# Expert products in one of four run-time widths, chosen by branches on TensorE

## The chip, the cores and the metric

The kernel runs on one core of a Trainium2 chip. The metric is device time in microseconds, lower is better; the time of the kernel before is the median of three runs. One more execution was recorded by the hardware profiler, and all rows below come from it.

## What is computed

A gated linear attention with a complex decay (4 batches, 8 heads, 768 steps, 48 values a head) gives 3072 rows of 384 values. A mixture of eight experts then takes each row to one expert, chosen by the largest of eight gate logits, and multiplies the expert's answer by two gates. The part that matters here:

```python
e_idx = np.argmax(logits, axis=1)
...
for e in range(E):
    mask = e_idx == e
    if not mask.any():
        continue
    h = np.maximum(x[mask] @ w1[e], 0.0)
    ye = h @ w2[e]
    out[mask] = gate_w[mask, None] * eom[mask, e, None] * ye
```

An expert has two matrices, `w1` of 384 x 1024 and `w2` of 1024 x 384. How many rows it gets is known only at run time.

## The kernel before

The program has two stages on one core. The first, the attention, lasts until some 278 us; it also routes the tokens. The second runs the eight experts one after the other (`experts`, L1125) and ends with the span.

**Places and capacities.** After most of the tokens are routed, the experts are ranked by how many tokens they have so far (`ranking`, L312), the fullest first. The expert at place n of this order gets room for `CAPS[n]` tokens (L24: 464, 440, 424, 416, 408, 400, 392, 384), whatever its number of tokens is in the end. Its tokens are gathered from DRAM into `rows` in four tiles (the last expert: three), so that token r of an expert lies in tile r mod 4. All products of place n stream `CAPS[n]` columns. `over` (L1390) compares the final counts with the capacities; if one is exceeded, a branch at the end of the program (L1411) enters a fallback, which the inputs here do not need. That branch is on all five engines, and each reads its word for it from `words` (L1410).

**One expert.** The 1024 hidden values are done in eight rounds `ft` of 128. Each float32 operand is split in a high and a low part, so a product is three matmuls on TensorE (high x high, low weight x high, high weight x low). A round has an up group, nine matmuls (3 x three parts of the 384 inputs) into one of two `up` banks (L1237), then ScalarE writes `hh` (relu, high part, L1241) and VectorE `hl` (low part, L1242). A down group of nine matmuls (L1174) adds the round into three `acc` banks; it is issued one round later, when `hh` and `hl` are there. After the eighth round the sums are copied to `yt`, and `put` (L1203) turns them back to rows: for each of four tiles three transposes into the single `yp` bank, `y` on ScalarE (times the gate, L1209), and an indirect DMA issued by GpSimd that scatters the rows (L1187). One tile is put in each of the next expert's rounds 1 to 4. The last expert computes its rows directly (`down_rows`, L1194), without `put`.

**Beside the products.** Each round also takes three steps of preparing the next expert (`ahead`, L1160): twelve steps split the weights, 128 x 512 each (ScalarE casts the high part, VectorE subtracts, L210 and L211), and wait for the weights' DMA through two `raw` buffers; three steps transpose the gathered rows into `xh` and `xl` (L1146 to L1148), in rounds 4 and 5.

**Order of work.** ScalarE and VectorE execute in the written order (`manual_schedule` with `by_hand`, L1408). The order on TensorE, SyncE and GpSimd in the expert stage is chosen by the framework's scheduler. In a round of the middle experts TensorE's order came out as up group, transposes if any, down group. In the written order a round has: up group, `hh`, `hl`, then one tile of `put` if there is one (L1244), the down group of the round before, then the three steps.

## Time and profile before

| what | value |
|---|---|
| median of 3 runs | 532.56 us (531.41 to 533.61) |
| profiled execution | 527.01 us |
| its span, first to last instruction | 525.3 us |
| TensorE matmuls busy | 489.0 us, 93% of the span |
| VectorE / ScalarE / GpSimd busy | 336.6 / 314.4 / 115.3 us |
| mean granted TensorE clock | 0.982 of full speed |

A busy share is a mean over stages with different limits. TensorE's matmuls are pipelined: one starts before the one ahead of it has ended, so what a matmul costs in a dense row is the distance between two starts, and a TensorE that is busy throughout can still be sped up by doing less. PEld is the loading of weights, which overlaps; PEldq, ACTq and the like are what an engine's sequencer does by itself, such as loads of registers and branches.

### The profile page before, as it was taken

The page shows a single profiled execution, that of the slowest core. Times are in us where ns is not written, and L with a number is a line of the kernel's source. Part 1 is how long each engine was busy: PE and PEld are TensorE (multiplying, and loading weights), DVE is VectorE, ACT ScalarE, POOL GpSimd, SP SyncE. Part 2 cuts the span into 40 slices and gives each one's busy share as a digit, 9 for nine tenths or more (in the row PEclk, how much of TensorE's full clock was granted, in tenths as well). Part 3 has the DMA queues.
Part 4 walks back from the last instruction along what each step waited for, and adds up shares of the span by engine and source line. Part 5 has one row for each costly group of instructions (what it writes and reads, how often), then busy time and mean ns, then how long its engine had stood idle before and what let it go on. Part 6 is the DMA issues. An engine that isn't in the chain of part 4 may idle for free.

```text
span 525.3 us, 10906 instructions
## 1 busy us (share of the span) xinstructions
PE 489.0 (93%) x4174; PEld 422.8 (80%) x4174; DVE 336.6 (64%) x777; ACT 314.4 (60%) x578; POOL 115.3 (22%) x134
## 2 busy tenths in 40 slices
PE   2799896999999999999999999999999999999992
PEld 0378574878777778778897889999999999999991
DVE  5679678979887988888867736354453636364220
ACT  7678677986869788756724436364453627264220
POOL 4002002020020203032320562413233322011112
PEclk9999989999999999999999999999999999999996
DMA  8764442526235321114425667445262635340001
GB/s 282 206 224 144 117 132 59 170 62 172 89 77 151 53 72 48 32 32 137 138 60 152 184 184 220 123 142 166 64 205 94 216 110 168 121 141 25 22 22 46
DMA packets 46898, 63.84 MB, mean 122 GB/s; under 512 B 11769, under 2 KB 38668, under 8 KB 46836
## 3 DMA queue, kind: packets, MB, share of 16 engines
q1 hardware_dynamic: 38708, 53.63, 33.7%
q0 software_dynamic: 8128, 9.42, 6.1%
q8 instruction: 35, 0.57, 0.5%
q14 instruction: 27, 0.22, 0.2%
HBM read 53.92 MB, written 9.88 MB: 121 GB/s over the span
## 4 chain that ended last, share of the span: by engine, by line
PE 65%; issue 16%; DVE 6%; ACT 5%; POOL 3%; DMA 3%; POOLq 0%; SPq 0%; DVEq 0%; ACTq 0%
PE up L1237 13%; PE acc L1174 12%; PE tr L94 7%; PE sc L664 6%; PE xo L678 4%; PE tr L245 4%; PE cs L574 4%; PE cs L521 3%; POOL out_dram L1187 3%; PE st L649 3%; PE xo L684 3%; PE st L644 1%; DMA carry<-ai 1%; DMA ar<-in_a_re_dram 1%; PE yp L94 1%
## 5 line engine op out<-in xcount | busy, mean ns | idle before, releaser
L1242 DVE SCALAR_TENSOR_TENSOR hl<-up,hh 128x464 fp32r<-128x464 f32 (+7 forms) x64 | 37.7, 590 | 72.8 <-ACT hh L1241 69.6
L1241 ACT ACTIVATE hh<-up 128x464 fp32r<-128x464 f32 (+7 forms) x64 | 33.0, 516 | 79.1 <-PE up L1237 76.4
L1237 PE MATMUL up<-xh,w1h 128*128 128x464 f32 (+7 forms) x192 | 68.7, 358 | 0.2 <-ACT xh L1024 0.2
L1237 PE MATMUL up<-xl,w1h 128*128 128x464 f32 (+7 forms) x192 | 67.7, 353 | 0.0
L1237 PE MATMUL up<-xh,w1l 128*128 128x464 f32 (+7 forms) x192 | 67.6, 352 | 0.0
L1174 PE MATMUL acc<-hh,w2h 128*128 128x464 f32 (+6 forms) x168 | 61.3, 365 | 0.0
L1174 PE MATMUL acc<-hl,w2h 128*128 128x464 f32 (+6 forms) x168 | 59.4, 353 | 0.0
L1187 POOL DMA_INDIRECT out_dram<-y,sid x28 | 31.7, 1133 | 125.7 <-ACT y L1209 122.7
L1174 PE MATMUL acc<-hh,w2l 128*128 128x464 f32 (+6 forms) x168 | 59.3, 353 | 0.0
L664 PE MATMUL sc<-qt,kt 96*128 96x128 f32 x384 | 52.5, 279 | 0.0
L664 PEld LDWEIGHTS sc<-qt,kt 96*128 96x128 f32 x384 | 47.2, 192 | 3.4 <-issue 1.8
L1118 POOL DMA_INDIRECT rows<-xd,sid x28 | 35.0, 1250 | 51.3 <-DVE hl L1242 25.7
L678 PE MATMUL xo<-scores,v 128*48 128x128 f32 x384 | 42.9, 278 | 0.3 <-issue 0.2
L211 DVE TENSOR_TENSOR w1l<-raw,w1h 128x512 fp32r<-128x512 f32 x48 | 30.7, 687 | 19.1 <-ACT w1h L210 19.1
L1064 POOL DMA_INDIRECT table<-entry,addr x20 | 27.0, 1348 | 53.0 <-DVE addr L1060 49.1
L544 POOL COPY rcs<-rcs 24x48 f32<-24x48 f32 (+2 forms) x10 | 6.0, 604 | 144.2 <-DMA rcs<-re 119.2
L211 DVE TENSOR_TENSOR w2l<-raw,w2h 128x512 fp32r<-128x512 f32 x48 | 30.6, 689 | 11.0 <-ACT w2h L210 10.8
L1237 PEld LDWEIGHTS up<-xl,w1h 128*128 128x128 f32 x192 | 36.1, 188 | 1.5 <-DVE xl L1025 0.4
L1237 PEld LDWEIGHTS up<-xh,w1h 128*128 128x128 f32 x192 | 36.1, 188 | 1.3 <-ACT xh L1024 0.4
L1237 PEld LDWEIGHTS up<-xh,w1l 128*128 128x128 f32 x192 | 36.2, 188 | 0.9
L684 PE MATMUL xo<-qt,state 96*48 96x128 f32 x320 | 36.5, 274 | 0.0
L665 DVE TENSOR_TENSOR scores<-sc,mask 128x512 f32<-128x512 f32 x48 | 32.7, 683 | 5.5 <-PE sc L664 5.1
(228 smaller groups left out, 1098.1 us busy)
## 6 DMA issues: line engine op xcount, KB each, us to landing
raw<-in_moe_w_dram SPq DMA_DIRECT2D x32, 768.0 KB
ar<-in_a_re_dram SPq DMA_DIRECT2D x24, 192.0 KB
ai<-in_a_im_dram SPq DMA_DIRECT2D x24, 192.0 KB
k<-in_k_dram SPq DMA_DIRECT2D x24, 192.0 KB
q<-in_q_dram SPq DMA_DIRECT2D x24, 192.0 KB
v<-in_v_dram SPq DMA_DIRECT2D x24, 192.0 KB
xd<-xn SPq DMA_DIRECT2D x24, 192.0 KB
rows<-xd,sid POOLq DMA_INDIRECT x28
```

Source lines behind the costliest of these rows:

```text
L94: return nc.tensor.transpose(out=out, in_=in_, identity=ident[p0:p0 + n, p0:p0 + n])
L211: nc.vector.tensor_tensor(out=lo[:, s], in0=raw[:, s], in1=hi[:, s].bitcast(F32), op=ALU.subtract)
L664: nc.tensor.matmul(sp[:, j * P:(j + 1) * P], r["kt"][:D2, h, :], r["qt"][:D2, h, :], start=True, stop=True)
L665: nc.vector.tensor_tensor(out=r["s"][:, 4 * hh:4 * hh + 4, :], in0=sp.rearrange("p (h t) -> p h t", t=P), in1=mask.unsqueeze(1).broadcast_ ...
L678: nc.tensor.matmul(op[u * DP:u * DP + D, j * P:(j + 1) * P], vt[c][:, h * D:(h + 1) * D], r["s"][:, h, :], start=True, stop=(cc == 0))
L684: nc.tensor.matmul(op[u * DP:u * DP + D, j * P:(j + 1) * P], xs[:D2, h * D:(h + 1) * D], r["qt"][:D2, h, :], start=False, stop=True)
L1118: ins = nc.gpsimd.indirect_dma_start(out=rows[e % 2][:n, i, :], out_offset=None, in_=xd[:known], in_offset=bass.IndirectOffsetOnAxis(ap=id ...
L1174: nc.tensor.matmul(accs[kt][:, :cap], w[:, cs], a, start=(ft == 0 and s == 0), stop=(ft == FT - 1 and s == 2))
L1187: ins = nc.gpsimd.indirect_dma_start(out=out, out_offset=bass.IndirectOffsetOnAxis(ap=id_of(e, i, n, loaded), axis=0), in_=y[:n, :], in_of ...
L1237: nc.tensor.matmul(up[:, :cap], w[:, kt, :], x[:, kt, :], start=(m == 0), stop=(m == 3 * KT - 1))
L1241: nc.scalar.activation(out=hh, in_=up[:, :cap], func=AF.Relu)
L1242: nc.vector.scalar_tensor_tensor(out=hl, in0=up[:, :cap], scalar=0.0, in1=hh.bitcast(F32), op0=ALU.max, op1=ALU.subtract)
```

## The change

For the second to the seventh expert, TensorE's up and down products stream one of four widths: the capacity, or 16, 32 or 48 columns less.

- `over`, which runs in round 4 of the first expert, computes for each place how many steps of 16 columns are free, cut to 0 to 3, in six VectorE operations, and leaves them in `spare`. TensorE loads the eight words into registers in round 6.
- Each group of products is written four times, one width each, inside two nested levels of `tc.If` on TensorE's register (`by_width`). An up group and the down group of the round before, where they are of one expert, share one such block of 18 products; where an expert begins, they are two blocks of nine.
- Since an expert's tokens lie in four parts, columns are left out at the end of each part: operand and bank are addressed as four pieces (`used`).
- From the second expert on TensorE keeps the written order: up and down products of a round, then the preparing steps' transposes, then one tile of `put`, which is now called after the three steps and not before them.
- The tile pools that rotate their buffers are replaced by tiles that are made once and taken in turn, in the same numbers.

ScalarE and VectorE still work on the whole capacity, and the last expert's widths stay.

```diff
+STEP = 16
+SPARE = 4
...
+            def used(t, n):
+                cap = t.shape[-1]
+                return t if n == cap else t.rearrange("p (i n) -> p i n", i=NS)[:, :, :n // NS]
+
+            def by_width(e, *products):
+                def go(lo, hi):
+                    if hi - lo == 1:
+                        for f in products:
+                            f(sizes[e] - lo * STEP)
+                        return
+                    mid = (lo + hi) // 2
+                    with tc.If(now["spare"][e] >= mid) as cmp:
+                        go(mid, hi)
+                    with cmp.Else():
+                        go(lo, mid)
+                go(0, SPARE if e in now["spare"] else 1)
+
+            def up_products(e, ft, up):
...
+                def go(n):
+                    m = 0
+                    for kt in range(KT):
+                        for w, x in ((w1h, xh), (w1l, xh), (w1h, xl)):
+                            nc.tensor.matmul(
+                                used(up[:, :sizes[e]], n), w[:, kt, :], used(x[:, kt, :], n), start=(m == 0),
+                                stop=(m == 3 * KT - 1))
+                            m += 1
+                return go
+
+            def down_products(e, accs, ft, hh, hl):
...
+                                used(accs[kt][:, :sizes[e]], n), w[:, cs], used(a, n), start=(ft == 0 and s == 0),
+                                stop=(ft == FT - 1 and s == 2))
...
             for e in range(E):
+                if loaded and e == 1:
+                    by_hand.enter_context(tc.manual_schedule(engines={mybir.EngineType.PE}))
...
                 for ft in range(FT):
-                    up = ps.tile([P, 512], F32, name="up")
...
+                    up = bank_of["up"].next()
+                    put_next = done
+                    before = prev
+                    if before is not None and before[0] == e:
+                        by_width(e, up_products(e, ft, up), down_products(*before))
+                    else:
+                        by_width(e, up_products(e, ft, up))
+                        if before is not None:
+                            by_width(before[0], down_products(*before))
+                    hh, hl = [t.next()[:, :cap] for t in hidden]
                     nc.scalar.activation(out=hh, in_=up[:, :cap], func=AF.Relu)
...
-                    next(done, None)
                     if prev is not None:
                         done = itertools.chain(done, down(*prev))
...
+                        if ft == 6:
+                            _, values = nc.values_load_multi_w_load_instructions(
+                                spare, engines=[mybir.EngineType.PE], min_val=0, max_val=SPARE - 1,
...
+                            now["spare"].update({n: values[n] for n in range(1, E - 1)})
                     for _ in range(2 if loaded and e == 0 else 3):
                         next(steps, None)
+                    next(put_next, None)
...
         nc.tensor.matmul(cp[:, :E], ones_b, run[:, NT, :], start=True, stop=True)
+        mine, left = pool.tile([1, E, E], F32, name="mine"), pool.tile([1, E], F32, name="left")
+        nc.vector.tensor_tensor(
+            out=mine, in0=is_at[0:1], in1=cp[0:1, :E].unsqueeze(1).broadcast_to([1, E, E]), op=ALU.mult)
+        nc.vector.tensor_reduce(out=left, in_=mine, axis=AX.X, op=ALU.add)
+        nc.vector.tensor_tensor(out=left, in0=caps[0:1], in1=left, op=ALU.subtract)
+        nc.vector.tensor_scalar(
+            out=left, in0=left, scalar1=1.0 / STEP, scalar2=0.5 / STEP - 0.5, op0=ALU.mult, op1=ALU.add)
+        nc.vector.tensor_scalar(out=left, in0=left, scalar1=ROUND, scalar2=-ROUND, op0=ALU.add, op1=ALU.add)
+        nc.vector.tensor_scalar(
+            out=spare, in0=left, scalar1=0.0, scalar2=float(SPARE - 1), op0=ALU.max, op1=ALU.min)
         nc.vector.tensor_tensor(out=more, in0=cp[:, :E], in1=cap_of, op=ALU.subtract)
```

## Rows read from the trace of the kernel before

**Rows 1.** The page: busy us by engine, and the granted clock in 40 slices.
```profile
PE 489.0 (93%) x4174; PEld 422.8 (80%) x4174; DVE 336.6 (64%) x777; ACT 314.4 (60%) x578; POOL 115.3 (22%) x134
...
PEclk9999989999999999999999999999999999999996
```
**Rows 2.** Busy us of each engine from 303 to 490 us, clock, DMA share, GB/s.
```profile
303.00:490.00 187.00, 187.00 (x1064) 181.50 (x1063) 89.76 (x151) 91.07 (x181) 51.91 (x46) 1.00 0.44 137
```
**Rows 3.** Timeline of PE: start us, us, line, operation; first of each run of products.
```profile
337.57 0.36 PE L1237 MATMUL up<-xh,w1h 128*128 128x440 f32 x1
...
341.17 0.35 PE L1237 MATMUL up<-xh,w1h 128*128 128x424 f32 x1
...
503.83 0.34 PE L1237 MATMUL up<-xh,w1h 128*128 128x384 f32 x1
...
508.58 0.34 PE L1200 MATMUL acc<-w2h,hh 128*128 128x384 f32 x1
```
**Rows 4.** Timeline of PE in the first expert's input: contiguous (L1013), four parts (L1001).
```profile
272.39 1.95 PE L1013 MATMUL sc<-ident,rows 116*128 116x116 f32 x16
274.18 0.50 PE L1013 MATMUL st<-ident,rows 116*128 116x116 f32 x3
...
277.09 0.27 PE L1001 MATMUL sc<-row,q 128*128 128x208 f32 x1
...
277.42 0.28 PE L1001 MATMUL st<-row,k 128*128 128x208 f32 x1
```
**Rows 5.** Loads of registers and branches (ns min/median/max, first and last start); PE's last product.
```profile
L332 SPq TENSOR_LOAD <-order x1: 981/981/981, 239.2 to 239.2; - x1
L1410 PEldq TENSOR_LOAD <-words x1: 484/484/484, 511.7 to 511.7; - x1
...
L1411 PEldq EVENT_SEMAPHORE  x2: 51/51/51, 516.2 to 516.4; - x2
...
L1411 SPq COMPARE_BRANCH  x1: 58/58/58, 468.0 to 468.0; - x1
L1411 PEldq COMPARE_BRANCH  x1: 3832/3832/3832, 512.3 to 512.3; - x1
...
L1411 ACTq COMPARE_BRANCH  x1: 50/50/50, 515.7 to 515.7; - x1
...
514.69 0.34 PE L1200 MATMUL acc<-w2h,hl 128*128 128x384 f32 x1
```
**Rows 6.** The page's DMA queues: packets, MB, share; the queue of TensorE's instructions.
```profile
q8 instruction: 35, 0.57, 0.5%
```
**Rows 7.** A small DVE operation (busy, mean ns), its timeline in `over`, the chain's down group.
```profile
L326 DVE TENSOR_TENSOR pair<-is_at,desc 128x64 f32<-128x64 f32 x1 | 0.2, 211 | 0.0
...
297.17 0.17 DVE L1395 TENSOR_TENSOR more<-yp,cap_of 128x8 f32<-128x8 f32 x1 [0.63 <-PE yp L1394]
...
299.93 0.64 DVE L1242 SCALAR_TENSOR_TENSOR hl<-up,hh 128x464 fp32r<-128x464 f32 x1 [0.23 <-ACT hh L1241]
...
303.05 1.90 PE acc L1174 x9
```
**Rows 8.** Timeline of one round of the third expert: last up product, `hh`, `hl`.
```profile
350.02 0.35 PE L1237 MATMUL up<-xl,w1h 128*128 128x424 f32 x1
...
350.41 0.53 ACT L1241 ACTIVATE hh<-up 128x424 fp32r<-128x424 f32 x1 [0.96 <-PE up L1237]
...
350.97 0.60 DVE L1242 SCALAR_TENSOR_TENSOR hl<-up,hh 128x424 fp32r<-128x424 f32 x1 [0.63 <-ACT hh L1241]
```
**Rows 9.** Who waited for whom, 303 to 490 us: us in total, times, longest.
```profile
ACT w1h L210 <- DMA raw<-in_moe_w_dram: 8.1, 6, 1.8
ACT w2h L210 <- DMA raw<-in_moe_w_dram: 7.9, 4, 3.5
```
**Rows 10.** Timeline of the fourth expert around its late weights: ScalarE, then TensorE.
```profile
388.77 1.67 ACT L210 CAST w2h<-raw 128x512 fp32r<-128x512 f32 x3 [3.54 <-DMA raw<-in_moe_w_dram]
...
390.35 0.43 PE L1237 MATMUL up<-xh,w1h 128*128 128x416 f32 x1
```

More of the change, by code (lines that the diff above doesn't have):

```diff
@@ L171, in tile_gated_attention_moe @@
     words = keep.tile([1, 2], I32, name="words")
+    spare = keep.tile([1, E], I32, name="spare")
     placed = keep.tile([P, E], F32, name="placed")
@@ L181, in tile_gated_attention_moe, with __init__, next @@
     assert KT * FH == TH * HD
+    class Turns:
+        def __init__(self, pool, name, shape, n, dt=F32):
+            self.tiles = [pool.tile(shape, dt, name=f"{name}{i}") for i in range(n)]
+            self.n = 0
+        def next(self):
+            self.n += 1
+            return self.tiles[(self.n - 1) % len(self.tiles)]
     def one(w, e):
@@ L1139, in transpose_x @@
                 xg, cap = rows[e % 2], sizes[e]
-                xh = xp.tile([P, KT, CAP], F32R, name="xh")[:, :, :cap]
-                xl = xp.tile([P, KT, CAP], F32R, name="xl")[:, :, :cap]
+                xh, xl = [t.next()[:, :, :cap] for t in part]
                 X[e] = xh, xl
                 for kt in range(KT):
-                    tp = ps.tile([P, 512], F32, name="xt")
+                    tp = bank_of["xt"].next()
                     for i, (t, n) in enumerate(tiles_at(e, cap, loaded)):
@@ L1151, in weights @@
             def weights(e):
-                W[e] = ready["set"] if loaded and e == 0 else weight_set((ready["pool"], wp)[e % 2])
+                W[e] = wsets[e % 2]
                 if e + 1 < E and e not in L:
@@ L1164, in ahead @@
                     yield from transpose_x(e)
-            def down(e, accs, ft, hh, hl):
+            def used(t, n):
[13 more added lines that the diff above has]
+                go(0, SPARE if e in now["spare"] else 1)
@@ new lines, in up_products @@
+            def up_products(e, ft, up):
+                half, c = divmod(ft, TH)
+                xh, xl = X[e]
+                w1h, w1l = [t.rearrange("p (k f) -> p k f", f=FH)[:, :, c * P:(c + 1) * P] for t in W[e][0][half]]
+                def go(n):
[7 more added lines that the diff above has]
+                return go
@@ L1176, in down @@
+            def down(e, accs, ft, hh, hl):
+                cap = sizes[e]
                 if ft < FT - 1:
                     return iter(())
-                yt = hp.tile([P, KT, CAP], F32, name="yt", bufs=1)[:, :, :cap]
+                yt = sums.next()[:, :, :cap]
                 for kt in range(KT):
@@ L1214, in experts @@
                 X[0], W[0], L[1] = ready["x"], ready["set"], ready["pieces"]
-                last = ready["lists"](lpool, lambda: ps.tile([P, 512], F32, name="yp", bufs=1))
+                last = ready["lists"](lpool, bank_of["yp"].next)
             else:
@@ L1248, in experts @@
                     if accs is None:
-                        accs = [ps.tile([P, 512], F32, name="acc", bufs=KT) for _ in range(KT)]
+                        accs = [bank_of["acc"].next() for _ in range(KT)]
                         if e == E - 1:
-                            accs += [ps.tile([P, 512], F32, name="xt") for _ in range(len(last_tiles) - KT)]
+                            accs += [bank_of["xt"].next() for _ in range(len(last_tiles) - KT)]
                     if e < E - 1:
@@ L1263, in experts @@
                         if ft == 4:
-                            over(lpool, lambda: ps.tile([P, 512], F32, name="yp", bufs=1))
+                            over(lpool, bank_of["yp"].next)
+                        if ft == 6:
+                            _, values = nc.values_load_multi_w_load_instructions(
+                                spare, engines=[mybir.EngineType.PE], min_val=0, max_val=SPARE - 1,
+                                skip_runtime_bounds_check_because="cut to the numbers from 0 to SPARE - 1")
+                            now["spare"].update({n: values[n] for n in range(1, E - 1)})
                     for _ in range(2 if loaded and e == 0 else 3):
                         next(steps, None)
+                    next(put_next, None)
                     if loaded and e == 0 and ft == 2:
@@ L1275, in experts @@
                     down_rows(e, accs, i, *h)
-                y = hp.tile([P, HD], F32, name="y", bufs=4)
+                y = done_rows.next()
                 if i % 2:
```

40 lines of the change are left out of this document (20 added, 20 removed).

## The prediction

> **What bounds the kernel now.** I read the page first. TensorE's row has 489.0 of 525.3 us busy, and its clock row shows full speed in nearly all of the span [rows 1]; since a busy PE is not yet PE at its peak, I went on to the stretch that the change touches. The table by stage gives 187.00 us of PE in the 187 us from 303 to 490 us (the second to the seventh expert), with VectorE and ScalarE at 90 and 91 us, and a granted clock of 1.00, the level of 2.4 GHz [rows 2]. The timeline then gives the distance from one start to the next, which is what a pipelined product costs: 18 products of 440 columns start between 337.57 and 341.17 us, 200.0 ns each; 27 of 384 columns between 503.83 and 508.58 us, 175.9 ns each [rows 3]. So the stage is a row of products without holes, and a column is worth (200.0 - 175.9)/56 = 0.43 ns. Whatever shortens a product there, and opens no hole, shortens the kernel.
>
> **Narrower products.** Which width is chosen follows from the inputs, by routing the reference's own inputs as its code does: with the experts in the kernel's order, the second to the seventh get 403, 406, 392, 388, 370 and 354 tokens against capacities of 440, 424, 416, 408, 400 and 392. That spares 2, 1, 1, 1, 1 and 2 steps of 16 columns, 128 columns in all. Each of these experts has 8 x (9 + 9) = 144 products, so 128 x 144 x 0.43 = **7.9 us** go, all on the path. The narrowest, 360 columns, would start every 166 ns, above the 112 ns that a product with 128 weight columns needs however few columns it streams [rows 4], so the weight load does not take over.
>
> **Four parts instead of one run.** Operand and bank are now walked in four pieces of 90 to 102 columns. The only products of before that write a bank in four parts are those of L1001, 208 columns: the first and the fourth of a run lie 0.33 us apart, 110 ns each, and the contiguous 116-column ones of L1013 start 112 ns apart (sixteen in 1.79 us) [rows 4]. On the line through 384 columns, 208 contiguous ones would cost 100 ns, so the price of the parts is between 0 and 10 ns a product, 0 to 8.6 us for all 864; nothing suggests a gain. I take 0, since L1001 is no slower than its neighbour, which has no parts. The Trainium skill speaks against this change here: "SBUF — State Buffer" (the passage on cachelines) says that any non-contiguous PSUM pattern slows matmuls significantly. No row agrees for pieces this long: twice the cost would have made L1001 200 ns, not 110.
>
> **Branches.** The 864 products stand in 54 groups (42 with 18, 12 with 9), each four times in the code. Per group TensorE meets two compares and one or two jumps. The nearest rows are the branches at the end of the program: 50 and 58 ns on ScalarE and SyncE, 3832 ns on TensorE, whose target lay far off behind the fallback code [rows 5]. They run ahead of the products: TensorE read its word at 511.7 us and branched at 512.3 us, while its last product started at 514.69 us [rows 5]. So some 2.95 us of queued work lie over a branch. Two or three short ones, 0.2 us, cost nothing under that cover; at 3.83 us each they would cost 3.83 - 2.95 = 0.88 us or more every time. I take the short price, as the longest skip here is two variants (some 72 instructions), unlike the one over the whole fallback. The code grows by 3 x 864 pairs, some 5,500 instructions with the jumps. Today 35 packets bring about 8,430 of them [rows 1, 6] (4174 pairs and some 80 others), 240 each, so 23 more come, one per 5.6 us in the stage; beside 0.5% of DMA time that is nothing.
>
> **The added load and the six small DVE operations** lie in the first expert. The load of the eight `order` words took SP 0.98 us [rows 5]; on TensorE it runs in the same cover, so 0. Six DVE operations of up to 0.21 us, some 1.2 us, come before L1395 at 297.17 us [rows 7], where DVE had just waited 0.63 us. The next `hl` ends at 300.57 us and moves by less than 1 us; its down group starts at 303.05 us [rows 7]. The transpose of `deep` behind them moves along, in a part whose order the scheduler still chooses: 0.
>
> **Written order on TensorE.** Each group now is up(ft), then down(ft-1), then the transposes; before, the transposes stood between. Their number and their returns to products are the same: 0. If the block is reported done only as a whole, `hh` starts one down group later. ScalarE and VectorE need 1.20 us from the last up product's end (350.02 + 0.35) to the end of `hl` (350.97 + 0.60) [rows 8]; the next group gives 9 + 2 products of 0.18 us less the 0.17 us overlap, 1.8 us. So 0.6 us remain, and still no hole. The replaced pools rotate through the same numbers of buffers: 0.
>
> **The step that moves.** Putting a finished tile (three transposes, ScalarE's `y`, POOL's scatter) used to be issued before the three weight casts of its round, and now after them. The scatter comes up to 1.7 us later, for which nothing waits, since the last expert follows. But `y` frees the only `yp` bank, and TensorE, now in written order, waits for it in front of the next up group. Three casts and a `y` take 1.67 + 0.57 = 2.24 us, and the next use of the bank comes about 4.6 us after the casts could start (a down group, transposes and a whole group, less `hh`: 1.6 + 0.3 + 3.3 - 0.6), so casts that wait up to 2.3 us for weights are covered. In the stage ScalarE waited ten times for weights, 16.0 us in all, at most 1.8 us for `w1h` and 3.5 us for `w2h` [rows 9]. The longest ended at 388.77 us [rows 10]. There three casts and a `y` behind them would end at 391.0 us, where TensorE, by then 0.6 us ahead of today's 390.35 us, wants the bank at 389.8 us: 1.2 us of hole. Faster products make every late weight later still. Bounds: 0 to 16 us; I take **+1.5 us**, near the lower end, as one wait alone is clearly above the cover.
>
> **Sum.** -7.9 + 1.5 = -6.4 us. The profiled execution took 527.01 us (span 525.3 us), 5.55 us below the median of the runs, 532.56 us; so 520.6 us for it and **526.2 us** for the median.
>
> **The rivals.**
> *Late weights reach TensorE through the bank.* The mechanism just priced, at 6 to 10 us in place of 1.5: 531 to 535 us, no change. For it: three of the four `w2h` waits average 1.5 us, and each expert gets 0.9 to 2 us shorter while its weights do not. Against it: the sum of waits is mostly time in which ScalarE had nothing else to do. Widths that are not narrower at all, for example because the counts read as zero steps, end here too.
> *Parts cost what the rows allow.* 8.6 us more: 534.8 us, and with a few late weights past 535.2 us, so slower. From 7.4 ns a product (6.4 us over 864) the gain is gone. The rule of "SBUF — State Buffer" in the Trainium skill would have it so.
> *Code arrives late.* TensorE jumps past code faster than it is fetched; each of the 32 packets of the stage is then missed once, at 0.88 us past the cover: 28 us, 554 us, slower. It decides when a jump meets a block that has not landed. For it: 3832 ns on TensorE's one branch. Against it: a group executes 36 of its 144 to 150 instructions, so a packet lasts 5.6 us on average. "Runtime: NRT & Kernel Launch" in the Trainium skill (instruction fetch mechanics) says that a taken branch stalls where its target is outside the current two pages; the far branch agrees, and by that rule the short ones here would be free.
> *Every join empties the queue.* If the arms' end or the next entry makes TensorE's sequencer wait for its own products, each of 54 groups pays the tail of a product (0.16 us), an event of 51 ns, the branches and a weight load (0.19 us), 0.5 us: 27 us, 553 us. For it: at the program's end two such events follow the branch [rows 5]. Against it: the arms hold equal numbers of products, so nothing has to be evened out.
>
> **How the numbers follow.** A measurement can tell 0.5%, 2.7 us. The forecast has 0.60 (holes of 0 to 5 us, 524.7 to 529.9 us), a still better one (no hole and a low draw, 522.5 to 524.7 us; the runs shown spread by 1.1 us either way) 0.07, late weights or unchanged widths 0.13, the parts 0.04, late code 0.08, emptied queues 0.08. So faster 0.67, same 0.13, slower 0.20. The range goes from 522.5 us to 535.2 us, the edge of no change, and leaves out the slower cases.
>
> **What would show it.** In the changed profile the up and down products of the second expert are 408 columns wide, some 186 ns apart, and those of the seventh 360 wide, some 166 ns; TensorE has holes only in front of `yp` transposes, with ScalarE's `y` as releaser, first of all in the fourth expert. Holes of 0.4 us or more in front of every up group would mean joins or code; wide spacing at the right widths, the parts; the old widths, that nothing was chosen. I am wrong if the stage from the second to the seventh expert is not 5 to 8 us shorter.

## The result and the profile after

The changed kernel takes 526.97 us (median of 6 runs, 525.91 to 528.24) against 531.98 us (530.15 to 534.06) for the kernel before on the same chip: ratio 0.9904, 95% interval 0.9875 to 0.9933, so 5.0 us less (3.6 to 6.6). The forecast was 526.2 us.

The profiled execution of the changed kernel took 527.06 us, like the one before (527.01 us), with the same span. That is chance: the attention of the one before ended early, so that its expert stage began at 278.00 us, the changed one's at 283.53 us; in the runs below, whose attention is the same, it began anywhere from 275.85 to 284.08 us. What the change did has to be read from the stage it touches. The page of the changed kernel (lines of engines, granted clock and the queue of TensorE's instructions; [rows 1, 6] before):

```profile
PE 486.3 (93%) x4174; PEld 421.6 (80%) x4174; DVE 338.0 (64%) x783; ACT 314.9 (60%) x578; POOL 116.7 (22%) x134
...
PEclk9999989999998999999999999999999999999996
...
q0 software_dynamic: 8128, 9.42, 6.3%
q8 instruction: 56, 0.92, 0.8%
```

The number of products is unchanged, and 21 packets of code came in addition, where 23 were expected.

The busy time by stretch, from the first up product of the second expert to that of the last; first the kernel before, whose PE is without a hole there as in [rows 2]:

```profile
309.66:486.70 177.04, 177.04 (x1008) 172.25 (x1007) 86.86 (x146) 88.34 (x176) 48.40 (x43) 1.00 0.43 137
```

The same stretch of the changed kernel:

```profile
315.27:486.84 171.57, 171.57 (x1009) 169.02 (x1008) 87.14 (x146) 88.49 (x176) 50.29 (x43) 1.00 0.48 144
```

Both are PE from end to end at full clock, and the stretch is **177.04 - 171.57 = 5.47 us** shorter. It is the measure of every run below, as it varies far less than the time of a whole execution (177.04 and 177.06 us below, where the products are the same). What the products look like in it (timeline of PE; first product of an up group of nine and of what follows it, for the second, the fifth and the seventh expert):

```profile
319.17 0.35 PE L1211 MATMUL up<-xh,w1h 128*128 128x408 f32 x1
...
320.87 0.35 PE L1225 MATMUL acc<-hh,w2h 128*128 128x408 f32 x1
...
406.48 0.35 PE L1211 MATMUL up<-xh,w1h 128*128 128x408 f32 x1
...
408.15 0.34 PE L1225 MATMUL acc<-hh,w2h 128*128 128x408 f32 x1
...
463.07 0.33 PE L1211 MATMUL up<-xh,w1h 128*128 128x360 f32 x1
...
464.58 0.33 PE L1225 MATMUL acc<-hh,w2h 128*128 128x360 f32 x1
```

The second expert's 408 columns, in four parts, come 1.70/9 = 189 ns apart; the fifth expert's 408, which is its whole capacity and so one run, 1.67/9 = 186 ns; the seventh's 360 columns, in parts, 168 ns. By the line of [rows 3] 408 and 360 columns should take 186 and 166. So a walk in parts costs something at 102 and 90 words a part. Medians of the others: 392 columns (parts of 98) 184 ns, by the line 179; 400 (parts of 100) and 384 (parts of 96) 183 and 176, by the line 183 and 176.

The widths that were chosen are 408, 392, 400, 408, 384 and 360, which fit 403, 392, 388, 406, 370 and 354 tokens: the ranking stands on fewer tokens than the prediction assumed (the first 14 of 24 tiles give this order), so the expert with 406 tokens has the fifth place. The number of columns spared is 128 all the same.

The branches, and the load of the eight steps (sequencer of TensorE: ns min/median/max, first and last start):

```profile
L1196 PEldq COMPARE_BRANCH  x153: 69/179/2412, 313.4 to 486.9; - x153
...
L1325 PEldq TENSOR_LOAD <-spare x1: 779/779/779, 312.5 to 312.5; - x1
```

They add up to 30.6 us of the sequencer's time (54 groups with two compares, 45 of them with a jump out of the arm), and no hole answers to them. In three successive groups of the second expert the branches run from 313.38 to 313.89, from 316.91 to 317.63 and from 319.96 to 320.76 us, and the first products start at 315.27, 319.17 and 322.82 us. So the queue covers 1.9 to 2.9 us, of which the branches use 0.5 to 0.8, and 1.4 to 2.1 us are left.

ScalarE's waits for weights from 303 to 490 us ([rows 9] before):

```profile
ACT w1h L223 <- DMA raw<-in_moe_w_dram: 10.5, 6, 2.0
...
ACT w2h L223 <- DMA raw<-in_moe_w_dram: 5.3, 6, 1.1
```

And the place of the predicted hole, the fourth expert's late weights (timeline, [rows 10] before):

```profile
389.01 1.66 ACT L223 CAST w2h<-raw 128x512 fp32r<-128x512 f32 x3 [0.85 <-DMA raw<-in_moe_w_dram]
...
390.57 0.57 ACT L1266 ACTIVATE y<-yp,gate 106x384 f32<-106x384 f32 x1
```

The weights that were 3.54 us late are now 0.85 us late, the `y` behind them ends at 391.14 us, and the next `yp` transposes start at 392.54 us: no hole.

### The profile page after: what moved, and what is told of

It is laid out like the page before. It is cut to its first block, busy times and chain, and to the rows that moved or that the text cites. A ratio compares the mean times of both kernels' runs of the same rounds, so it can differ in the third digit from the quotient of the medians.

```text
span 525.3 us, 11082 instructions
## 1 busy us (share of the span) xinstructions
PE 486.3 (93%) x4174; PEld 421.6 (80%) x4174; DVE 338.0 (64%) x783; ACT 314.9 (60%) x578; POOL 116.7 (22%) x134
## 3 DMA queue, kind: packets, MB, share of 16 engines
q0 software_dynamic: 8128, 9.42, 6.3%
## 4 chain that ended last, share of the span: by engine, by line
PE 60%; issue 16%; DVE 7%; DMA 6%; ACT 5%; POOL 3%; SPq 1%; POOLq 0%; DVEq 0%; ACTq 0%
PE up L1211 13%; PE acc L1225 12%; PE tr L96 6%; PE sc L677 5%; PE xo L691 4%; PE tr L258 4%; PE cs L587 4%; PE cs L534 3%; POOL out_dram L1244 3%; PE st L662 2%; PE xo L697 2%; DMA carry<-ai 2%; DMA ar<-in_a_re_dram 1%; PE st L657 1%; PE yp L96 1%
## 5 line engine op out<-in xcount | busy, mean ns | idle before, releaser
L1211 PE MATMUL up<-xh,w1h 128*128 128x408 f32 (+5 forms) x192 | 69.5, 362 | 0.2 <-ACT xh L1037 0.2
L1211 PE MATMUL up<-xh,w1l 128*128 128x408 f32 (+5 forms) x192 | 66.5, 346 | 0.0
L1211 PE MATMUL up<-xl,w1h 128*128 128x408 f32 (+5 forms) x192 | 66.5, 346 | 0.0
L1244 POOL DMA_INDIRECT out_dram<-y,sid x28 | 33.6, 1199 | 126.1 <-ACT y L1266 123.5
L1225 PE MATMUL acc<-hh,w2h 128*128 128x408 f32 (+5 forms) x168 | 58.4, 348 | 0.0
L1225 PE MATMUL acc<-hl,w2h 128*128 128x408 f32 (+5 forms) x168 | 58.4, 347 | 0.0
L1225 PE MATMUL acc<-hh,w2l 128*128 128x408 f32 (+5 forms) x168 | 58.4, 347 | 0.0
L557 POOL COPY rcs<-rcs 24x48 f32<-24x48 f32 (+2 forms) x10 | 4.8, 484 | 143.8 <-DMA rcs<-re 118.9
L587 PE MATMUL cs<-ai,tri_t 128*128 128x384 f32 x48 | 24.0, 590 | 13.1 <-DVE ai L569 7.3
```

Of the source, the lines that this page charges most:

```text
L587: nc.tensor.matmul(tp[:, :HD], tri_t, fr, start=True, stop=first or not plain)
L1211: nc.tensor.matmul(used(up[:, :sizes[e]], n), w[:, kt, :], used(x[:, kt, :], n), start=(m == 0), stop=(m == 3 * KT - 1))
L1225: nc.tensor.matmul(used(accs[kt][:, :sizes[e]], n), w[:, cs], used(a, n), start=(ft == 0 and s == 0), stop=(ft == FT - 1 and s == 2))
L1244: ins = nc.gpsimd.indirect_dma_start(out=out, out_offset=bass.IndirectOffsetOnAxis(ap=id_of(e, i, n, loaded), axis=0), in_=y[:n, :], in_of ...
```

## The experiments

2.4 of the 7.9 us of narrower products are missing. Theories: parts (the four pieces in which an operand is walked) that do not fit groups of four words cost it; the branches, the written order or the moved step cost it; columns are worth less. "Stretch" is the one above; ratios are to the kernel before on the same chip. Each group of runs shared one chip.

| run | stretch, us | ratio to before (95%) |
|---|---|---|
| before / changed | 177.04 / 171.57 | 0.9904 (0.9875 to 0.9933) |
| columns_alone | 168.82 | 0.9792 (0.9736 to 0.9848) |
| full_width | 177.06 | 0.9992 (0.9952 to 1.0031) |
| no_branches | 171.79 | 0.9927 (0.9890 to 0.9964) |
| aligned_parts | 172.65 | 1.0037 (1.0003 to 1.0072) |
| put_first | 172.08 | 0.9909 (0.9858 to 0.9961) |
| rank_order | 170.09 | 0.9854 (0.9798 to 0.9911) |
| rank_put_first | 171.99 | 0.9888 (0.9843 to 0.9934) |
| rank_step8 | 176.55 | 0.9916 (0.9873 to 0.9958) |
| rank_step8_again | 174.10 | 0.9918 (0.9887 to 0.9950) |
| branch_per_three | 201.85 | a single execution, 553.16 us against 528.39 |

### The columns alone

```diff
-CAPS = (464, 440, 424, 416, 408, 400, 392, 384)
+CAPS = (464, 408, 392, 400, 408, 384, 360, 384)
```

in the kernel before.

> The kernel before with the capacities 464, 408, 392, 400, 408, 384, 360, 384: the widths that the changed kernel chose on these inputs, fixed in the program, contiguous, without parts, branches, written order or moved step. From the second expert's first up product to the last expert's first one the trace gives 177.04 us before and 171.57 us after (-5.47 us), where 128 columns by 144 products by 0.43 ns would be -7.9 us; 2.4 us are missing. Theory (parts that do not begin on a multiple of four words cost 4 to 5 ns a product, about 1.9 us in all): the whole 7.9 us come here, the stretch is 169 to 169.5 us, 408 columns 185 to 186 ns apart, 392 columns 178, 360 columns 166, and the time some 2.4 us below the changed kernel's. Rival 1 (branches and written order cost the 2.4 us): the same here. Rival 2 (columns are worth less than 0.43 ns, or narrower products meet another limit): 171 to 172 us here as well.

Measured: 168.82 us, 8.22 us less than before, with 408 columns 185 to 186 ns apart, 392 at 178 and 360 at 165. The columns are worth what the prediction gave them, and the loss comes with the way the changed kernel picks them. The time fell by 11.0 us (ratio 0.9792), 2.7 more than the stretch; where these come from stands at the end.

### Branches without spared columns, columns without branches

full_width:

```diff
-                            f(sizes[e] - lo * STEP)
+                            f(sizes[e])
```

> The changed kernel with the full capacity in every arm: branches, four variants, load, written order and moved step kept, no column spared and no parts (the operands are contiguous). Theory: the stretch is that of the kernel before, 177.0 us within 0.4, and so is the time, within 0.5%. Rival 1 (branches and order cost what is missing): 179 to 179.5 us, 2.4 us over the kernel before. Rival 3 (the moved step opens holes through the yp bank): 177.5 us or more, with holes in front of yp transposes.

no_branches (and no load of `spare` on TensorE):

```diff
+WIDTHS = (464, 408, 392, 400, 408, 384, 360, 384)
...
-                go(0, SPARE if e in now["spare"] else 1)
+                for f in products:
+                    f(WIDTHS[e] if loaded else sizes[e])
```

> The changed kernel with the same widths fixed in the program: no branches, one variant of each group, no load on TensorE; four parts, written order and moved step kept. Theory: nothing is gained, the stretch is 171.6 us within 0.4, 408 columns in parts stay 189 ns apart and 360 columns 168 to 169, the time equals the changed kernel's within 0.5%. Rival 1 (branches): 169 to 170 us, and 2 us less time. If only the written order or the moved step costs, the spacing falls to 186, 178 and 166 ns and the stretch still stays near 171.6 us, with holes.

Measured: 177.06 us against 177.04 before, and 171.79 us against 171.57 changed. Branches, four variants of the code, load, written order and moved step together cost nothing that shows; taking the branches away brings nothing. Rival 1 falls. The loss is, for the most part, in the spacing.

### Which parts cost, and on which side

aligned_parts: the parts begin on multiples of four words, and their widths stay (the gathers and loads of the places follow the layout).

```diff
+LAYOUT = (464, 448, 432, 416, 416, 400, 400, 384)
...
-        sizes = CAPS if loaded else [CAP] * E
+        sizes = LAYOUT if loaded else [CAP] * E
...
-                            f(sizes[e] - lo * STEP)
+                            f((CAPS[e] if loaded else sizes[e]) - lo * STEP)
```

> The changed kernel with the operands and banks laid out for 464, 448, 432, 416, 416, 400, 400 and 384 columns, so that each of the four parts begins on a multiple of four words (strides of 112, 108, 104, 104, 100, 100 words); the widths multiplied stay 408, 392, 400, 408, 384 and 360. Theory: 408, 392 and 360 columns come 186, 178 and 166 ns apart as the contiguous ones do, and the stretch is 169.5 to 170 us, 1.7 us less than the changed kernel's; the fourth expert's 408 columns, now in parts of 102 at a stride of 104, stay at 186. Rival (any walk in parts costs 4 ns): spacing 189, 183 and 169 ns as in the changed kernel, the fourth expert's 408 rise to 189 too, and the stretch is 172 us. If the length of a part and not its beginning is what counts, the spacing stays as in the changed kernel and the fourth expert's rises as well; then a layout with lengths in multiples of four is to be tried.

Measured: 408 columns at 191.5 ns, 392 at 186, 360 at 170, and the fifth expert's 408 (the expectation calls it the fourth), now in parts of 102, rose to 188; the stretch is 1.1 us longer than the changed kernel's. The theory of the beginnings falls; what the expectation named last is left, that the length counts. So the lengths were varied, without branches:

```diff
+            def width(e, ft):
+                return min(FIRST[e] + 8 * (ft // 2), CAPS[e]) if 0 < e < E - 1 else CAPS[e]
...
                 def go(n):
+                    n = width(e, ft) if loaded else n
                     m = 0
```

> The changed kernel with fixed widths and no branches, and the up products of one expert in up to four widths, two groups each: parts of 102, 104, 106 and 108 words at a stride of 110 (second expert), 98 to 104 at 106 (third), 98 to 104 at 104 (fourth), 94 to 100 at 100 (sixth), 90 to 96 and 98 contiguous at 98 (seventh). The run with aligned beginnings has ruled the beginning out (408 columns 191 ns, 392 columns 186 ns, 360 columns 170 ns there). Theory now: what counts is the length of a part; one that is no multiple of four words costs as if filled up to the next, so that 408 columns cost what 416 do (189.7 ns by the line through 440 and 384), 392 what 400 do (182.8), 376 what 384 do (175.9), 360 what 368 do (169.0), 424 what 432 do (196.6), and each full pair comes at the same spacing within 1 ns. Rival A (groups of four words that a part touches, beginning included): parts of 104 at a stride of 110 cost what 424 columns do, 193.1 ns, and parts of 92 at 98 what 376 do, 172.5. Rival B (a fixed 3 to 4 ns for every walk in parts): 416 in parts at 193 ns, 432 at 200, 384 at 179, 368 at 172.

Measured, as medians of 16 distances of up products each; "line" is the contiguous price by [rows 3] for the columns, and for the words of all aligned groups of four that the parts touch:

| stride, part | columns | line, ns | four-word groups x 4 | line, ns | measured, ns |
|---|---|---|---|---|---|
| 110, 102 | 408 | 186.2 | 416 | 189.7 | 189.5 |
| 110, 104 | 416 | 189.7 | 424 | 193.1 | 191.5 |
| 110, 106 | 424 | 193.1 | 432 | 196.6 | 198 |
| 110, 108 | 432 | 196.6 | 440 | 200.0 | 198.5 |
| 106, 100 | 400 | 182.8 | 408 | 186.2 | 186 |
| 106, 104 | 416 | 189.7 | 424 | 193.1 | 193 |
| 104, 98 | 392 | 179.4 | 400 | 182.8 | 182.5 |
| 104, 100 | 400 | 182.8 | 400 | 182.8 | 184 |
| 100, 96 | 384 | 175.9 | 384 | 175.9 | 176 |
| 98, 92 | 368 | 169.0 | 376 | 172.5 | 172.5 |
| 98, 96 | 384 | 175.9 | 392 | 179.4 | 179.5 |

Rival A of that run holds: what is paid for are the groups of four words that a part touches, at its beginning and at its end: all rows are within 2 ns, and so are the seven other shapes of the run. The theory of the length alone fails where a part of whole fours begins in the middle of one (stride 106 with 104: 193, not 189.7). The "SBUF — State Buffer" page of the Trainium skill (the passage on cachelines) gives SBUF lines of 16 bytes, four float32 values, each change of line to be paid: these rows agree. In aligned_parts the parts of 98 and 102 words at strides of 108 and 112 came 2 to 3 ns above even this count; that remains open.

one_side_in_parts: the up products only write in parts, the down products only read in parts.

```diff
-                                used(up[:, :sizes[e]], n), w[:, kt, :], used(x[:, kt, :], n), start=(m == 0),
+                                used(up[:, :sizes[e]], n), w[:, kt, :], x[:, kt, :n], start=(m == 0),
...
-                                used(accs[kt][:, :sizes[e]], n), w[:, cs], used(a, n), start=(ft == 0 and s == 0),
+                                accs[kt][:, :n], w[:, cs], used(a, n), start=(ft == 0 and s == 0),
```

> As the run on lengths, but the up products read the rows contiguously and only write their bank in parts, and the down products read the hidden values in parts and write their banks contiguously; so the columns of the tokens don't match and the output of the second, third, fourth, sixth and seventh expert is not the reference's. If the price lies in the write: up products as in the run on lengths (408 columns 189 to 190 ns, 392 183, 376 176, 360 169), down products at the contiguous spacing (408 185 to 186, 392 178, 376 172, 360 165). If it lies in the read: the other way about. If either side in parts is enough: both at 189, 183, 176 and 169.

The second expert's 408 columns there (timeline of PE, first product of a group of nine and the first one after it; first the up group, then the down group):

```profile
311.43 0.35 PE L1207 MATMUL up<-xh,w1h 128*128 128x408 f32 x1
...
313.10 0.36 PE L1222 MATMUL acc<-hh,w2h 128*128 128x408 f32 x1
...
336.29 0.35 PE L1222 MATMUL acc<-hh,w2h 128*128 128x408 f32 x1
...
338.00 0.34 PE L1207 MATMUL up<-xh,w1h 128*128 128x392 f32 x1
```

Written in parts and read in one run: 1.67/9 = 186 ns, the contiguous price. Read in parts and written in one run: 1.71/9 = 190 ns, the price of the parts. The medians of the other widths say the same (written in parts 177.5 ns for 392 columns and 163.5 for 360; read in parts 183 to 184 and 169). The price lies in the read of the streamed operand alone. The sentence on PSUM in that passage of the Trainium skill ("SBUF — State Buffer"), that any non-contiguous pattern there slows products significantly, does not agree with these rows: four pieces of 90 to 102 words in a bank cost nothing.

### The moved step

```diff
                         out=hl, in0=up[:, :cap], scalar=0.0, in1=hh.bitcast(F32), op0=ALU.max, op1=ALU.subtract)
+                    next(put_next, None)
...
-                    next(put_next, None)
```

> The changed kernel with the step that puts a finished tile issued before the weight casts of its round again, as in the kernel before. The prediction had the moved step at +1.5 us (bounds 0 to 16). Theory (the cover holds): nothing changes, the stretch is 171.6 us within 0.4, the time within 0.5% of the changed kernel's. If the moved step costs what was predicted: 170.1 us and 1.5 us less.

Measured: 172.08 us, 0.3 to 0.5 us more than with the moved step (171.57 and 171.79). The prediction's sign was wrong, as far as one profiled execution of each kernel shows; the times (ratios 0.9909 and 0.9904) do not tell the two apart. Timeline of this run, fourth expert: ScalarE's casts, `hh`, then VectorE's `hl` and the down product that waits for it:

```profile
389.55 1.66 ACT L223 CAST w2h<-raw 128x512 fp32r<-128x512 f32 x3 [2.94 <-DMA raw<-in_moe_w_dram]
...
391.11 0.51 ACT L1301 ACTIVATE hh<-up 128x416 fp32r<-128x416 f32 x1
...
392.01 0.58 DVE L1302 SCALAR_TENSOR_TENSOR hl<-up,hh 128x416 fp32r<-128x416 f32 x1
...
392.65 0.45 PE L1225 MATMUL acc<-hl,w2h 128*128 128x400 f32 x1 [0.30 <-DVE hl L1302]
```

With the step first, the weights of `w2h` are 2.94 us late here (0.85 us in the changed kernel); the casts end at 391.21 us, `hh` and VectorE's `hl` stand behind them and the subtractions, and TensorE waits for `hl`. That in the changed order the casts, earlier by one `y`, free the `raw` buffers and start the next transfer earlier would explain it, but was not isolated.

### Columns in the order of rank

A version without parts: the copies out of the banks put the columns of places 1 to 6 in the order of the tokens' rank, so that fewer tokens are a shorter run, and turn them back in `yt`.

```diff
+                return [t.rearrange("p (n i) -> p n i", i=NS) for t in ranked] + [by_slot.rearrange("p (i n) -> p n i", i=NS)]
...
-                return t if n == cap else t.rearrange("p (i n) -> p i n", i=NS)[:, :, :n // NS]
+                return t if n == cap else t[:, :n]
```

> The changed kernel, but the columns of the second to the seventh expert stand in the order of the tokens' rank, so that the narrower products are one contiguous run; ScalarE's and VectorE's copies out of the banks (of the transposed rows, and of the finished sums) put them into that order and back, reading or writing four runs in turn. Branches, widths and written order as in the changed kernel. Theory: products at the contiguous spacing (408 columns 185 to 186 ns, 392 178, 360 165), no holes, the stretch from the second to the last expert's first up product 169.2 us within 0.4 against 171.6 in the changed kernel, and 2 to 2.4 us less time than it. Rival (the copies that walk across four runs become slow and late): TensorE waits for the transposed rows or for the one yp bank, with holes in front of the first up products of an expert or of yp transposes; at twice the time for each such copy the stretch would be over 171 us.

Measured: 170.09 us, 1.48 us less than the changed kernel, and 0.5 us above the expected band. The products are at the contiguous spacing (408: 185, 392: 179, 360: 165). The missing half us is one hole (timeline, seventh expert):

```profile
462.28 1.67 ACT L223 CAST w1h<-raw 128x512 fp32r<-128x512 f32 x3 [2.40 <-DMA raw<-in_moe_w_dram]
...
463.85 0.57 ACT L1273 ACTIVATE y<-yp,gate 100x384 f32<-100x384 f32 x1
...
464.47 0.54 PE L96 MATMUL yp<-ident,yt 128*100 128x128 f32 x3 [0.35 <-ACT y L1273]
```

This is the prediction's mechanism of the moved step in a kernel whose experts are shorter. Only the copies that write `yt` in four runs became slower (lines of that run; the changed kernel's copies to `yt` on ScalarE took 513 ns on average):

```profile
L1172 ACT CAST xh<-xt 128x440 fp32r<-128x440 f32 (+6 forms) x21 | 9.8, 503 | 17.0 <-PE xt L96 17.0
...
L1247 ACT COPY yt<-acc 128x464 f32<-128x464 f32 (+5 forms) x12 | 10.4, 870 | 1.7 <-PE acc L1231 1.1
```

With the put step ahead of the casts as well:

> The run with the columns in the order of rank (170.1 us from the second to the last expert's first up product), and the put step back ahead of the weight casts. There one hole of 0.5 us stood at 464.47 us: the casts, 2.4 us late for their weights, delayed the y behind them, and TensorE waited for the one yp bank. Theory: that hole goes, 169.6 us within 0.3, unless hh is the one that is late behind casts elsewhere (as with the put step first in the changed kernel, one hole of 0.46 us); the time equals that of the run in rank order within 0.5%. If the moved step costs the predicted 1.5 us: 168.6 us.

Measured: 171.99 us. The hole at the `yp` bank went, but three of 0.5 us came where `hh` or `hl` was late behind `w2h` casts (`w2h` waited up to 3.6 us), and one of 0.8 us from a jump of 3517 ns, although there are only four variants. So the moved step stays.

### Branches beyond their cover

branch_per_three: a choice for every three products, 288 in place of 54.

```diff
-                go(0, SPARE if e in now["spare"] else 1)
+                for product in products:
+                    for kt in range(KT):
+                        go(0, SPARE if e in now["spare"] else 1)
```

> The changed kernel with its widths chosen anew for every three products (up or down, one block of 128 rows) in place of every group of 9 or 18: 288 choices in place of 54, the same products. In the changed kernel the two compares and the jumps of a group are done 1.4 to 2.1 us before the first product of the group starts, and the 153 branches of the stage take 30.6 us of the sequencer's time, 0.57 us a group. Theory (the branches are hidden because a group holds 1.8 to 3.3 us of products): with only 0.55 us of products behind each choice of 0.4 to 0.6 us the sequencer, which must also hand out six instructions, falls behind; the stretch grows by 5 to 60 us over 171.6. Rival (branches cost no time whatever lies behind them): 171.6 us within 0.4.

Measured (branches of the run, ns min/median/max):

```profile
L1195 PEldq COMPARE_BRANCH  x816: 69/176/1260, 308.7 to 514.6; - x164
```

The stretch grew by 30.3 us. Branches are free only as long as the queue covers them. The fifth expert, whose arm stands last in the code and needs no jump out of it, lost 0.7 us (29.73 against 29.05 us); the others lost 5.4 to 6.5 us, 0.11 to 0.14 us for each of their 48 choices. So two compares are nearly free even here, and the jump out of an arm is what costs. The fifth expert is also the only one here that is not walked in parts, but that is not it: the fourth and the sixth, whose parts cost nothing (183 and 176 ns for 400 and 384 columns), lost 5.6 and 5.4 us.

A fifth variant, on top of the order of rank:

```diff
-STEP = 16
-SPARE = 4
+STEP = 8
+SPARE = 5
```

> The run with the columns in the order of rank, with steps of 8 columns and five widths in place of steps of 16 and four: 408, 392, 392, 408, 376 and 360 columns, 16 columns fewer in the stage, a fifth variant of each group and up to three compares a group in place of two. Theory: 16 columns by 144 products by 0.43 ns = 1.0 us less than in rank order, so 169.1 us within 0.4 for the stretch; the third compare stays hidden. Rival (the fifth variant's code or the third compare is no longer covered): 170 us or more.

Measured: ratio 0.9916 (0.9873 to 0.9958), the stretch 176.55 us, with TensorE standing still before the fifth expert; the ten products behind that stop had a granted clock of 0.53, about the level of 1.2 GHz. I read the stop as a late transfer of weights.

> The run in rank order with steps of 8 columns and five widths once more: in its first profile one transfer of weights was so late that TensorE stood still for 2.8 us at 408.97 us and then had ten products at half the clock, so that it told nothing on the 16 columns. Theory: 16 columns by 144 products by 0.43 ns = 1.0 us less than in rank order, 169.1 us within 0.4 for the stretch, if no weights are late; experts that are shorter while their weights are not make each late transfer count more, and where one is late again the spare columns are lost to it. Rival (the fifth variant's code or the third compare is no longer covered): 170 us or more with holes of several hundred ns at the starts of groups and none in front of casts or yp transposes.

Measured: the same stop at the same place, and 174.10 us. It was no transfer. The branches from 399 to 406 us in that run:

```profile
L1202 PEldq COMPARE_BRANCH  x6: 69/210/5264, 399.8 to 405.9; - x6
```

and its timeline of PE, the last product before the stop and the first after it:

```profile
402.74 0.34 PE L1231 MATMUL acc<-hl,w2h 128*128 128x392 f32 x1
405.63 0.45 PE L1217 MATMUL up<-xh,w1h 128*128 128x408 f32 x1 [2.55 <-issue]
```

One jump began at 399.76 us and took 5264 ns; it ended at 405.02 us, two more compares at 405.58 us, and the first product started at 405.63 us, 2.7 us later than the usual 0.18 us behind the product before. So 3.1 of the 5.8 us were covered by queued work. With five variants 19 of 198 jumps took 0.66 to 5.3 us here (18, of up to 5.5 us, in the first run); with four, 1 of 153 in the changed kernel (2412 ns at 453.9 us, wholly covered) and 1 or 2 of 153 in the other five runs. These are jumps to code that has not landed, as the packets of the queue of TensorE's instructions show. In this run one of 16384 bytes lies inside the long jump, from 402.66 to 403.62 us (that queue's line for the window from 402.6 to 403.7 us):

```profile
q8 instruction: 1, 0.02, 5.4%
```

The jump ended 1.4 us after it. The same holds everywhere: all 61 branches of TensorE's sequencer, in the 14 traces, that took 0.6 us or more, the far branch at the end of the program among them, ended 1.2 to 1.6 us after such a packet had landed; of the 2083 shorter ones 7% ended 1.3 to 1.55 us after one. The place is one of the code, too: all six runs with four variants of a group of 9 or 18 products have such a jump 21.6 to 22.3 us into the sixth expert. "Runtime: NRT & Kernel Launch" of the Trainium skill (Instruction fetch mechanics) has such a stall for targets outside the two pages at hand; the stall agrees with these rows; that two pages are the limit no row shows. Why the packet of the longest jump started only 2.9 us after the jump stays open. The expected 169.1 us and the 174.1 us measured differ by this hole, two more where TensorE waited for nothing but its own sequencer (0.5 us at 374.35 us behind a jump of 3190 ns, and some 0.4 us at 388.62 us) and three waits at the `yp` bank (some 1.4 us in all).

## Why the prediction came out right, point by point

The total is right within 0.8 us, and the stage is 5.5 us shorter where 6.4 were summed, inside the stated 5 to 8. Two of its terms were wrong and cancelled, so it is in part luck that the sum came out. That the total came closer than the gain (5.0 us, where 6.4 were summed) is luck as well: the kernel before came out at 531.98 us, not at the 532.56 us that the sum started from.

- **Bound and value of a column: right.** The stage was a row of products, and 128 columns gave 8.2 us when spared alone (7.9 predicted).
- **Parts: wrong, 0 taken.** The step that failed is "I take 0, since L1001 is no slower than its neighbour, which has no parts": L1001 has parts only in the bank that it writes and reads its operand in one run, and at 110 ns it is at the price of 128 weight columns anyway. It said nothing on the side that costs. By touched groups of four the second, third and seventh expert pay for 8 columns more each: 24 x 144 x 0.43 ns = 1.5 us. Undoing the parts brought 1.48 us, hole included, so between 1.5 and 2.0 us. The rival of the parts took the rule on banks ("SBUF — State Buffer" in the Trainium skill) at 8.6 us: written in four parts, products came 186 ns apart, the contiguous price. The line of four words, in the same passage of the Trainium skill, does agree, on the reading side.
- **Moved step: wrong in sign.** +1.5 us were taken; undoing it cost 0.3 to 0.5 us, in one profiled execution each. The failed step is the lateness of the weights, taken over unchanged from [rows 9, 10]: in the new order the longest wait for `w2h` was 1.1 us, not 3.5, and behind casts of 0.85 us lateness the `y` ends 1.4 us before it is wanted. The chain itself (casts, `y`, `yp` bank, TensorE) is real: 0.35 us in rank_order.
- **Branches: right that they are hidden, wrong in the price.** 0.5 to 0.8 us a group instead of 0.2 us, under a cover of 1.9 to 3.1 us (2.95 predicted). The margin was a factor of three to four, not of fifteen. What used it up was not the short branches but late code: the prediction's rival was the right mechanism with the wrong frequency, 1 or 2 long jumps a run with four variants, not one for each packet, and 18 or 19 with five. Even with four one of them once left a hole (0.8 us in rank_put_first).
- **Emptied queues, written order, load, DVE operations: right at 0.** full_width has them all, and its stretch equals that of the kernel before within 0.02 us; the first expert, in which the load and the DVE operations lie, takes 31.72 us against 31.66. `hh` did not wait for the whole group: in one the last up product ends at 336.72 us and `hh` starts at 336.75 us, with nine down products still to come.
- **Widths:** 408 at the second expert and 360 at the seventh came as predicted, the third and the fifth the other way about, since the ranking stands on fewer tokens than the prediction's order (14 of the 24 tiles give the order that was run, 20 the predicted one); the sum is the same.
- **The rest, placed but open:** columns_alone and the changed kernel differ by 2.75 us. By the distances from start to start, summed over the stretch, the 864 products take 1.99 us of it (159.64 against 157.65 us; the parts), and the 141 transposes among them 0.76 us (11.92 against 11.17 us). Part of that comes with the written order, since full_width's transposes take 11.77 us and those of the kernel before 11.37 us; there the products give the 0.4 us back. What makes the transposes longer was not tried.

The fastest version that still chooses its widths at run time was rank_order: 1.48 us less in the stretch than the changed kernel. Its ratio to before, 0.9854, and the changed kernel's, 0.9904, have overlapping intervals, so in the whole time the gain is not shown.

## What to carry to other kernels

Branches on TensorE are free while queued products outlast them: compare the sequencer's time a group with the distance from the last compare to the first product, and know that a shorter group can end it (30.3 us for choices of three products), and so can more code: with one more variant 18 or 19 jumps in place of 1 or 2 waited for code that had not landed. When an operand is cut into pieces, count the groups of four words that the pieces touch on the reading side, or let an engine with time to spare pack it into one run. A null price taken from a row that is limited by something else is not a price.

## What was not expected of the hardware

- The streamed operand is paid for by aligned groups of four words touched, in steps of 0.43 ns x 4 (18 shapes within 2 ns; two in aligned_parts 2 to 3 ns above); the bank's pieces cost nothing (186 ns written in parts, 190 ns read in parts, 408 columns).
- A compare or jump of TensorE's sequencer takes 69 to 424 ns in the changed kernel, but a few take 0.6 to 5.5 us, 1.2 to 1.6 us past the landing of a packet of code; with five variants in place of four there were 18 or 19 of them in place of 1 or 2.
- The end after the last scatter differed with the rows of a tile. In the changed kernel (tiles of 110, 106, 104, 102, 100 and 98 rows from the second to the seventh expert) the issue of the last scatter ends at 516.94 us, 8.4 us before the end of the span, as in the kernel before; q0 moved 8128 packets. The page of columns_alone (102, 98, 100, 102, 96 and 90 rows), where that issue ends at 508.96 us:

```profile
span 513.8 us, 10906 instructions
...
q0 software_dynamic: 6208, 9.39, 6.2%
```

and of aligned_parts (112, 108, 104, 104, 100 and 100 rows), where it ends at 514.99 us:

```profile
span 528.3 us, 11081 instructions
...
q0 software_dynamic: 5824, 9.39, 5.9%
```

So 4.8 and 13.3 us pass to the end, at nearly the same bytes. The difference lies in two closing instructions of GpSimd's sequencer, behind the last packet: the longest DRAIN of columns_alone, of the changed kernel and of aligned_parts

```profile
L1467 POOLq DRAIN  x3: 46/102/723, 512.2 to 513.5; - x3
...
L1542 POOLq DRAIN  x3: 46/103/2928, 521.6 to 525.1; - x3
...
L1543 POOLq DRAIN  x3: 46/103/6930, 520.5 to 528.0; - x3
```

and the INC_SWDGE_SEM ahead of it (0.36, 0.90 and 1.88 us). All twelve runs with 8128 packets, the kernel before among them, have 2.93 and 0.90 us. So columns_alone ends 2.75 us earlier by these two, which is what it gained beyond its stretch, and aligned_parts 4.98 us later, which uses up the 4.4 us of its stretch and leaves some 1.4 us of the 2.0 us that it lost unexplained. What sets their length was not tried.
